# Conversion stages in separate slots of a product step, bank sums ahead of curves, and casts handed out around the bank copies

## The chip, the cores and the metric

One core of one Trainium2 chip runs the whole program in one launch. The metric is the device time of that launch in microseconds: the median of the runs. A profiled execution stands beside it, from which all rows are read.

## What is computed

Attention over 4 batches, 8 heads, 576 positions and a head size of 64, with a learned bias of the position, then two dense feed-forward blocks ("MoE" in the code) over the 2304 tokens. All weights are float64 in memory.

```python
scores = scale * q @ k^T + bias            # bias: a small MLP of log distances
x = softmax(scores) @ v                    # -> 2304 x 512
h = x @ moe_w_in                           # 512 -> 1024
solu = h * softmax(h)
x = (solu - mu) / sqrt(var + 1e-6) * g_ln @ moe_w_out      # 1024 -> 512
h = x @ moe2_w_in                          # 512 -> 2048
g = where(h >= 1, h, where(h <= -1, 0, (h + 1)**2 / 4))
out = g @ moe2_w_out                       # 2048 -> 512
```

## The kernel before

Three stages follow each other: attention (to about 355 us), the first MoE (to about 576 us), the second MoE. Every float32 operand of a matmul is split in a high and a low part, and three matmuls make one product. Each engine runs its instructions in the order in which the code emits them, and waits at the first that isn't ready; the order below is written out by hand with generators (`step(g, n)` emits the next n pieces of one).

**Conversion of the second MoE's weights** (`split_pairs`, L659). A piece is a block of 128 x 512 float64 numbers. It becomes float32 in four stages, one per `step(bw)`. Stage 1: three VectorE operations on the raw bits (L691 to L695). Stage 2: ScalarE makes the exponent (L699). Stage 3: VectorE puts in the sign (L703), one multiply makes the number (L706), and the raw load of the next piece but one is issued on SyncE (L667). Stage 4: ScalarE casts the high half (L713, L717, L726); where the piece is the second of an input pair, four VectorE subtractions (L678) make the combinations that seven products in place of eight need. Low halves and two more casts (L673, L734, L735) are kept in the list `late` and go out at the head of later stages 1 and 4 or behind a stage 2; each low half is stored to memory by SyncE. Twenty pieces (k-rows s = 0 to 4) are converted in the first MoE, with the multiply and most low halves on GpSimd; twelve (s = 5 to 7) in the second MoE, with all of it on VectorE.

**First MoE.** 18 tiles of 128 tokens. Tile i: `emit_h(i)` multiplies by w_in (24 matmuls), `split_x(i + 2)` splits a later tile's input (ScalarE L542, GpSimd L543), `emit_post(i)` is softmax and norm in steps over VectorE, ScalarE and GpSimd (L577 maximum, L578 exponential, L580 to L582, L587 squares, L589, L592 power on GpSimd, L594 and L595, the last one emitted in the next tile), `emit_lt(i - 2)` transposes (ScalarE L822, VectorE L826), `emit_o` multiplies by w_out (48 matmuls, from tile 4 on). The result of `emit_o` lies in the one PSUM buffer ps_x until ScalarE copies it to os (L842); the next tile's `emit_o` can't begin before. From tile 4 on four stages go out per tile, all ahead of `emit_o`, and odd tiles from 5 on emit four more behind it. From tile 11 on `first_x2` prepares the seven combinations of the first tokens' x2, one or two parts a tile (ScalarE L759, GpSimd L760).

**Second MoE.** 24 steps n = 0 to 23 in five legs of 5, 5, 8, 3 and 3 steps (`plan`: leg, token block p, weight row s, first and last step of a leg). A step makes seven products in the order SEQ = 1, 2, 6, 5, 7, 3, 4, six matmuls each (`emit_m`, L969), into two PSUM banks ab in turn; between them go the output matmuls of step n - 1 (`unit`, L1008, six behind each of the first six products). Four blocks 11, 22, 12, 21 of h come out of the banks: ScalarE keeps bank copies (`keep`, L935), VectorE makes the sums of 11, 22 and 12 (`summed`, tile cs, L940) behind products 2, 7 and 3. A bank is free for its next product only when its sum or copy is done. Each block then goes through `relu` (ScalarE L944), `curve` (two VectorE operations, L948 and L949) and `split_g` (ScalarE L955, VectorE L956). Before: in step n the code emits one stage in the place of product 2 (the fourth of a piece) and three in that of product 5, except in the last step of legs 0 to 3. In the place of product 3 curve 22 goes out before sum 12.

In the last step of a leg (and the first of the next) the x2 halves of the next leg are cast (L1026) and their low halves made (L1029); `sums_x2` (L1023) prepares four differences of the loaded tiles st, one after product 6 and one after product 3 in each step but the first. In a leg's first step the six result banks of the leg are copied out or added (`evac`, L988 to L993) and sent to memory, and behind that SyncE issues the loads of st (L754).

## Time and profile before

| | us |
|---|---|
| median of 3 runs | 996.57 |
| lowest, highest | 995.03, 1000.17 |
| the profiled execution | 1000.56 |
| its span, first to last instruction | 998.6 |
| TensorE busy in the span | 930.2 (93%) |
| VectorE busy | 725.9 (73%) |
| ScalarE busy | 616.8 (62%) |
| GpSimd busy | 255.2 (26%) |
| mean granted TensorE clock | 0.977 |

A matmul's end is modelled, so the share of TensorE says little by itself; what counts is where it stands idle or runs at the low clock. The clock has two levels, 1.2 and 2.4 GHz, and the granted clock of a stretch is the mean of them as a share of the higher one. "Idle before, releaser" in a row is the time that the engine stood idle ahead of an instruction and what ended it.

### The profile page before, as it was taken

To read this page: it belongs to the slowest core of one execution; us is meant where nothing else is said; L and a number is where in the kernel's file an instruction comes from. 1 tells how busy PE (TensorE), PEld (TensorE's weight loads), DVE (VectorE), ACT (ScalarE), POOL (GpSimd) and SP (SyncE) were. 2 spreads that over 40 slices of the span, in tenths; PEclk is the share of its full clock that TensorE was granted. 3 is DMA by queue.
4 is the path that set the end of the run, shared out by engine and by line. 5 is a ranking of instruction groups with operands and counts; after the bars stand their busy time and mean duration, and the time that the engine had idled before them with its cause. 6 is when DMAs were issued, how large, how long until landed. Compare 5 with 4: busy or idle time off the path is not lost.

```text
span 998.6 us, 16911 instructions
## 1 busy us (share of the span) xinstructions
PE 930.2 (93%) x6052; PEld 788.8 (79%) x6052; DVE 725.9 (73%) x1540; ACT 616.8 (62%) x1290; POOL 255.2 (26%) x229
## 2 busy tenths in 40 slices
PE   8789999999999999989989989998998899999996
PEld 4148878877788889879878977887887778888885
DVE  8988888888887367777777157787677665576764
ACT  6988888989899665666566334554445334454541
POOL 1026656565654123534464300000000000000000
PEclk9999999999999999999989989999999899999999
DMA  5893653843741002543743776849455665348442
GB/s 162 269 290 130 207 173 124 251 130 138 232 145 38 1 22 95 200 161 127 237 163 137 249 258 202 303 138 331 154 169 195 227 211 177 113 122 262 143 155 95
DMA packets 101351, 173.14 MB, mean 173 GB/s; under 512 B 10450, under 2 KB 65234, under 8 KB 101268
## 3 DMA queue, kind: packets, MB, share of 16 engines
q1 hardware_dynamic: 96000, 165.70, 50.4%
q10 hardware_dynamic: 4900, 4.72, 1.4%
q0 software_dynamic: 368, 1.64, 0.5%
q8 instruction: 48, 0.79, 0.3%
q14 instruction: 35, 0.29, 0.1%
HBM read 125.48 MB, written 46.54 MB: 172 GB/s over the span
## 4 chain that ended last, share of the span: by engine, by line
PE 37%; DVE 8%; issue 6%; POOL 5%; ACT 4%; DMA 3%; SPq 1%; ACTq 0%; POOLq 0%; DVEq 0%
PE acc L1008 14%; PE ab L969 14%; PE ps_x L837 4%; PE ps_s L559 3%; POOL wp L706 2%; PE ps_s L837 1%; DMA part_d<-ob 1%; ACT wp L699 1%; DMA st<-x_d 1%; DVE wp L703 1%; POOL xl L543 1%; DVE cs L940 1%; DVE raw L694 1%; POOL wd L673 1%; DMA pt<-part_d 1%
## 5 line engine op out<-in xcount | busy, mean ns | idle before, releaser
L1008 PE MATMUL acc<-wo,gh 128*128 128x512 f32 x576 | 181.8, 397 | 0.4 <-DVE ob L993 0.4
L421 DVE CUSTOM_DVE_ANT_0 e<-ps_s,bt 128x576 f32<-128x576 f32 x144 | 107.2, 753 | 26.8 <-PE ps_s L415 23.7
L1008 PEld LDWEIGHTS acc<-wo,gh 128*128 128x128 f32 x576 | 108.2, 191 | 15.0 <-DVE ob L993 0.8
L436 ACT ACTIVATE e<-e,su 128x576 f32<-128x576 f32 x144 | 112.1, 779 | 8.7 <-DVE su L421 7.9
L1008 PE MATMUL acc<-wo,gl 128*128 128x512 f32 x288 | 115.7, 402 | 0.0
L415 PE MATMUL ps_s<-kh,sq 128*128 128x288 f32 x320 | 102.1, 336 | 6.7 <-DVE su L421 6.3
L969 PE MATMUL ab<-x2d,wr 128*128 128x384 f32 x288 | 90.7, 356 | 12.7 <-DVE cs L940 11.8
L482 ACT COPY pt<-ps_t 128x512 f32<-128x512 f32 x144 | 83.0, 577 | 20.1 <-PE ps_t L481 19.5
L481 PE MATMUL ps_t<-ident,e 128*128 128x128 f32 x576 | 88.7, 277 | 3.1 <-ACT pt L482 2.8
L415 PE MATMUL ps_s<-kl,sq 128*128 128x288 f32 x320 | 89.9, 297 | 0.0
L944 ACT ACTIVATE ga<-cs,half_c 128x384 f32<-128x384 f32 x72 | 44.4, 617 | 72.0 <-DVE cs L940 71.2
L837 PE MATMUL ps_x<-lh,woh 128*128 128x256 f32 x256 | 75.2, 294 | 12.3 <-ACT os L842 12.3
L956 DVE TENSOR_TENSOR gl<-ga,gh 128x384 fp32r<-128x384 f32 x96 | 53.1, 553 | 42.1 <-ACT gh L955 39.8
L935 ACT COPY pk<-ab 128x384 f32<-128x384 f32 x96 | 45.4, 473 | 60.8 <-PE ab L969 60.6
L513 PE MATMUL ps_x<-pt,v 128*64 128x256 f32 x640 | 78.0, 385 | 0.6 <-ACT pt L482 0.6
L955 ACT CAST gh<-ga 128x384 fp32r<-128x384 f32 x96 | 49.3, 514 | 47.0 <-DVE ga L949 47.0
L481 PEld LDWEIGHTS ps_t<-ident,e 128*128 128x128 f32 x576 | 67.8, 141 | 12.9 <-issue 5.8
L837 PE MATMUL ps_x<-ll,woh 128*128 128x256 f32 x256 | 73.8, 288 | 0.0
L837 PE MATMUL ps_x<-lh,wol 128*128 128x256 f32 x256 | 73.7, 288 | 0.0
L948 DVE SCALAR_TENSOR_TENSOR ga<-ga 128x384 f32<-128x384 f32 x96 | 53.3, 555 | 27.2 <-ACT ga L944 25.7
L969 PEld LDWEIGHTS ab<-x2d,wr 128*128 128x128 f32 x288 | 56.4, 198 | 20.5 <-DVE cs L940 16.2
L415 PEld LDWEIGHTS ps_s<-kh,sq 128*128 128x128 f32 x320 | 61.2, 191 | 12.0 <-DVE su L421 8.3
(199 smaller groups left out, 2320.5 us busy)
## 6 DMA issues: line engine op xcount, KB each, us to landing
wr<-wi_d SPq DMA_DIRECT2D x168, 256.0 KB, 3.5
stg<-in_qk_dram SPq DMA_DIRECT2D x30, 640.0 KB, 3.9
raw<-in_w2nd_dram SPq DMA_DIRECT2D x32, 512.0 KB, 4.0
wi_d<-wd SPq DMA_DIRECT2D x24, 512.0 KB, 4.0
bias_d<-ow SPq DMA_DIRECT2D x36, 295.5 KB, 3.7
wo_d<-wd SPq DMA_DIRECT2D x16, 512.0 KB, 2.9
wo<-wo_d SPq DMA_DIRECT2D x16, 512.0 KB, 5.1
st<-x_d SPq DMA_DIRECT2D x16, 384.0 KB, 5.8
```

What stands on the lines that cost most here:

```text
L415: nc.tensor.matmul(sc[:, hf, 0:HS], lhsT=l, rhs=r, start=j == 0, stop=j == len(parts) - 1)
L421: nc.vector.tensor_tensor_reduce(out=halves(e), in0=sc[:, :, 0:HS], in1=halves(b_t[hp, n]), scale=-1.0 / float(D) ** 0.5, scalar=3.0e38, o ...
L436: nc.scalar.activation(out=e, in_=e, func=ACTF.Exp, scale=-1.0, bias=su[:, n:n + 1], accum_out=su[:, 9 + n:10 + n])
L481: nc.tensor.transpose(tp[:, kt * 128:(kt + 1) * 128], e[:, c0:c0 + 128], ident)
L482: nc.scalar.copy(out=pt[:, 4 * h:4 * h + 4, 128 * o:128 * o + 128], in_=tp.rearrange("p (a b) -> p a b", a=4))
L513: nc.tensor.matmul(x[64 * h:64 * h + 64, o0:o0 + w], lhsT=v[:, kt, 64 * h:64 * h + 64], rhs=r, start=kt == 0, stop=kt == 4, skip_group_che ...
L837: nc.tensor.matmul(ob[:, a * 256:(a + 1) * 256], lhsT=l, rhs=r[:, f, :], start=f == 0 and j == 0, stop=f == K1 - 1 and j == 2,)
L948: nc.vector.scalar_tensor_tensor(out=a, in0=a, scalar=1.0, in1=a, op0=ALU.min, op1=ALU.mult)
L955: nc.scalar.copy(out=gh, in_=a)
L956: nc.vector.tensor_tensor(out=gl, in0=a, in1=gh.bitcast(F32), op=ALU.subtract)
L969: nc.tensor.matmul(d, lhsT=l, rhs=r[:, kk], start=q in (1, 2, 5) and kk == 0 and m == 0, stop=kk == 1 and m == 2, skip_group_check=True,)
L1008: nc.tensor.matmul(d, lhsT=l, rhs=r, start=first and m == 0, stop=last and m == 2, skip_group_check=True)
```

## The change

First MoE: six stages go out per tile from tile 4 on, four ahead of `emit_o` (behind the last part of the previous norm, behind the transposes' casts, behind L582, behind the low halves of the transposes) and two behind it; the burst of odd tiles is gone. The pieces come in another order: input pairs and the first output rows first, the second output rows (s, 3) last. In `first_x2` three `yield`s move, so that no part of a tile has two long GpSimd operations, except the last.

Second MoE: a piece's four stages go out one by one: stage 1 behind sum 22 (product 7), stage 2 behind curve 12 (product 4), stage 3 behind curve 11 in the next step (product 2), stage 4 behind the split of 11 (product 5). `conv` leaves out the last steps of legs 0 to 2 for a piece's begin, so that their stages 3 and 4 are those of the step before, and a leg's first step has stages 1 and 2 alone. Sum 12 is emitted ahead of curve 22. The differences of x2 go out once a step, in leg 3 twice.

```diff
@@ first_x2
         part(7, rb, nc.gpsimd)
+        yield
         xl2[6], xh2[4], xl2[4] = slot3("c")
         part(5, ra, nc.gpsimd)
-        yield
         sub(rb, l3, ra)
         yield
         part(6, rb, nc.gpsimd)
         sub(ra, l2, rb)
         yield
+        part(4, ra, nc.gpsimd)
+        yield
         xh2[1], xh2[2], xh2[3] = slot3("d")
         part(1, l1, nc.gpsimd)
-        part(4, ra, nc.gpsimd)
         yield
         part(2, l2, nc.gpsimd)
-        yield
         part(3, l3, nc.gpsimd)
@@ first MoE, once
-            bw = split_pairs([(s, k) for s in range(NPA) for k in range(4)], wd, 4, nc.gpsimd)
+            order = [(s, k) for s in range(3) for k in range(3)] + [(s, k) for s in (3, 4) for k in (0, 1)]
+            order += [(s, 2) for s in (3, 4)] + [(s, 3) for s in range(NPA)]
+            bw = split_pairs(order, wd, 4, nc.gpsimd)
@@ first MoE, a tile
         step(lt)
         if i >= 4:
             step(bw)
-        step(bp, 2)
-        drain(lt)
         step(bp)
         if i >= 4:
             step(bw)
-        bl = bp
-        if 4 <= i < NTT - 1:
+        step(bp)
+        drain(lt)
+        if i >= 4:
             step(bw)
+        step(bp)
         if i >= 4:
             emit_o((i - 4) // 2, i % 2)
-        if i % 2 == 1 and i > 4:
-            step(bw, 4)
+            step(bw, 2)
+        bl = bp
@@ second MoE
+    def conv(n):
+        return 0 <= n < NS - 1 and (plan[n][0] > 2 or not plan[n][4])
...
                     relu((n, 11))
-                    if n > 0 and swap != 0:
+                    curve((n, 11))
+                    if conv(n - 1):
                         step(bw)
-                    curve((n, 11))
...
                 split_g((n, 11))
-                if swap != 0:
-                    step(bw, 3)
+                if conv(n - 1):
+                    step(bw)
...
                 relu((n, 22))
+                if conv(n):
+                    step(bw)
             elif q == 3:
+                summed((n, 12), d, k_t[6])
                 curve((n, 22))
-                summed((n, 12), d, k_t[6])
                 split_g((n, 22))
                 relu((n, 12))
-                if not head:
+                if not head and g == 3:
                     step(xs)
             else:
                 c_t[n, 21] = keep(d)
                 curve((n, 12))
+                if conv(n):
+                    step(bw)
```

What this does to an engine's queue is seen at three places. VectorE, step 1 of the second MoE, from the split of block 11 on, before (L940 are sums 22 and 12, L948 and L949 curve 22, the rest a conversion's low half, stages 1 and 3):

```order
L956 TENSOR_TENSOR gl<-ga,gh 128x384
L673 TENSOR_TENSOR wd<-wp_7005,wd 128x512
L691 TENSOR_SCALAR wp_7150<-raw_6953 128x512
L694 SCALAR_TENSOR_TENSOR raw_6953<-raw_6953,wp_7150 128x512
L695 TENSOR_SCALAR wp_7150<-raw_6953 128x512
L703 SCALAR_TENSOR_TENSOR wp_7150<-raw_6953,wp_7150 128x512
L706 TENSOR_TENSOR wp_7150<-raw_6953,wp_7150 128x512
L940 TENSOR_TENSOR cs<-ab_6948,pk 128x384
L948 SCALAR_TENSOR_TENSOR ga<-ga 128x384
L949 TENSOR_TENSOR ga<-ga,cs 128x384
L940 TENSOR_TENSOR cs<-ab_6947,pk 128x384
```

The same place in the changed kernel, where the lines of the second MoE are two higher (L942 are the sums):

```order
L958 TENSOR_TENSOR gl<-ga,gh 128x384
L942 TENSOR_TENSOR cs<-ab_6948,pk 128x384
L673 TENSOR_TENSOR wd<-wp_7019,wd 128x512
L691 TENSOR_SCALAR wp_7170<-raw_6953 128x512
L694 SCALAR_TENSOR_TENSOR raw_6953<-raw_6953,wp_7170 128x512
L695 TENSOR_SCALAR wp_7170<-raw_6953 128x512
L942 TENSOR_TENSOR cs<-ab_6947,pk 128x384
L950 SCALAR_TENSOR_TENSOR ga<-ga 128x384
L951 TENSOR_TENSOR ga<-ga,cs 128x384
```

Sum 22 now follows the split, the conversion's first stage stands between the two sums, its third has left, and curve 22 stands behind sum 12. ScalarE in tile 8 of the first MoE, from the end of the tile before to the bank copy os, before:

```order
L726 CAST wd_5312<-wp_5299 128x256
L542 CAST xh<-xb_1419 128x512
L578 ACTIVATE eb,stb<-ps_s,stb 128x1024
L594 ACTIVATE stb<-stb 128x1
L595 ACTIVATE scb<-scb,stb 128x1024
L822 CAST lh<-ps_t 128x4x128 x2
L699 ACTIVATE wp_5354<-wp_5354,exp_c 128x512
L734 CAST wd<-wd 128x512
L735 CAST wd<-wd 128x512
L587 ACTIVATE eb,stb<-scb,stb 128x1024
L713 CAST wd<-wp_5354 128x512
L842 COPY os<-ps_x 128x512
```

And in the changed kernel:

```order
L713 CAST wd<-wp_5247 128x512
L542 CAST xh<-xb_1419 128x512
L578 ACTIVATE eb,stb<-ps_s,stb 128x1024
L594 ACTIVATE stb<-stb 128x1
L595 ACTIVATE scb<-scb,stb 128x1024
L822 CAST lh<-ps_t 128x4x128 x2
L699 ACTIVATE wp_5358<-wp_5358,exp_c 128x512
L587 ACTIVATE eb,stb<-scb,stb 128x1024
L717 CAST wd<-wp_5358 128x512
L842 COPY os<-ps_x 128x512
L843 DMA x_d<-os 128x2x256
L699 ACTIVATE wp_5448<-wp_5448,exp_c 128x512
```

The two casts L734 and L735 have left this tile, a piece's cast still stands ahead of os, and the next piece's exponent stands behind it. GpSimd in the same tile, before (L706 multiplies, L543 and L673 low halves, L592 the norm's power):

```order
L706 TENSOR_TENSOR wp_5299<-raw_5121,wp_5299 128x512
L543 TENSOR_TENSOR xl<-xb_1419,xh 128x512
L592 TENSOR_TENSOR stb<-stb,mhalf 128x1
L706 TENSOR_TENSOR wp_5354<-raw_5243,wp_5354 128x512
L543 TENSOR_TENSOR xl<-xb_1419,xh 128x512
```

And changed:

```order
L706 TENSOR_TENSOR wp_5247<-raw_5115,wp_5247 128x512
L543 TENSOR_TENSOR xl<-xb_1419,xh 128x512
L673 TENSOR_TENSOR wd<-wp_5247,wd 128x512
L706 TENSOR_TENSOR wp_5358<-raw_5222,wp_5358 128x512
L592 TENSOR_TENSOR stb<-stb,mhalf 128x1
```

The tile's multiply has moved ahead of the norm's power, with a low half ahead of it.

## Rows read from the trace of the kernel before

**Rows 1.** The page's first part: busy us, share of the span, instructions of each engine.

```profile
PE 930.2 (93%) x6052; PEld 788.8 (79%) x6052; DVE 725.9 (73%) x1540; ACT 616.8 (62%) x1290; POOL 255.2 (26%) x229
```

**Rows 2.** The chain that ended last: start us, us, what it was.

```profile
415.17 5.45 PE ps_s L559 x24
...
652.77 1.39 PE acc L1008 x6
...
902.31 2.08 PE ab L969 x12
```

**Rows 3.** Stretches of steps: length, busy (instructions) by engine, PEclk, DMA share, GB/s.

```profile
575.84:588.28 12.44, 8.73 (x44) 7.91 (x43) 7.12 (x13) 4.77 (x10) 0.00 (x0) 0.87 0.56 187
588.28:641.72 53.44, 50.08 (x234) 43.29 (x235) 39.57 (x73) 22.72 (x45) 0.00 (x0) 0.97 0.77 264
641.72:657.47 15.75, 15.75 (x78) 14.02 (x79) 11.57 (x19) 8.93 (x17) 0.00 (x0) 1.00 0.77 257
657.47:747.84 90.37, 83.80 (x391) 72.20 (x391) 68.89 (x125) 43.21 (x83) 0.00 (x0) 0.96 0.61 201
747.84:840.52 92.68, 84.96 (x391) 73.57 (x391) 63.27 (x113) 39.80 (x77) 0.00 (x0) 0.94 0.61 200
840.52:887.44 46.92, 46.92 (x235) 42.04 (x235) 26.54 (x47) 20.74 (x39) 0.00 (x0) 1.00 0.42 134
503.00:552.00 49.00, 42.41 (x259) 38.79 (x259) 36.27 (x66) 32.65 (x55) 26.57 (x20) 0.90 0.41 150
```

**Rows 4.** TensorE's waits, whole span: us in total, times, longest us.

```profile
PE ab L969 <- DVE cs L940: 19.9, 17, 3.7
PE ps_x L837 <- ACT os L842: 12.3, 5, 4.6
```

**Rows 5.** Timeline, TensorE in step 1: products 7, 4, then product 1 of step 2.

```profile
599.72 1.21 PE L969 MATMUL ab<-x2b,wr 128*128 128x384 f32 x6
...
604.87 1.33 PE L969 MATMUL ab<-x2c,wr 128*128 128x384 f32 x6
607.24 0.44 PE L969 MATMUL ab<-x2d,wr 128*128 128x384 f32 x1 [1.04 <-DVE cs L940]
```

**Rows 6.** Timeline, VectorE in step 1, from product 7 on.

```profile
599.93 0.68 DVE L673 TENSOR_TENSOR wd<-wp,wd 128x512 fp32r<-128x512 f32 x1
...
602.93 0.69 DVE L703 SCALAR_TENSOR_TENSOR wp<-raw,wp 128x512 uint32<-128x512 uint32 x1 [0.79 <-ACT wp L699]
...
604.27 0.55 DVE L940 TENSOR_TENSOR cs<-ab,pk 128x384 f32<-128x384 f32 x1
...
606.63 0.55 DVE L940 TENSOR_TENSOR cs<-ab,pk 128x384 f32<-128x384 f32 x1
```

**Rows 7.** Timeline, VectorE in steps 4 to 6, where legs change.

```profile
647.82 0.95 DVE L1029 TENSOR_TENSOR x2a<-st,x2d 128x768 fp32r<-128x768 f32 x1
...
663.01 0.42 DVE L678 TENSOR_TENSOR wd<-wd,wp 128x256 f32<-128x256 f32 x1
...
676.82 0.69 DVE L993 COPY ob<-acc 128x512 f32<-128x512 f32 x1 [1.03 <-DMA part_d<-ob]
...
686.12 0.96 DVE L1023 TENSOR_TENSOR st<-st,st 128x768 f32<-128x768 f32 x1 [2.77 <-DMA st<-x_d]
```

**Rows 8.** Timeline, GpSimd and ScalarE at the end of tile 8.

```profile
432.89 0.93 POOL L592 TENSOR_TENSOR stb<-stb,mhalf 128x1 f32<-128x1 f32 x1 [8.13 <-DVE stb L589]
433.79 1.37 POOL L706 TENSOR_TENSOR wp<-raw,wp 128x512 f32<-128x512 f32 x1
435.19 0.62 ACT L713 CAST wd<-wp 128x512 fp32r<-128x512 f32 x1 [2.57 <-POOL wp L706]
435.72 0.58 ACT L842 COPY os<-ps_x 128x512 f32<-128x512 f32 x1
```

**Rows 9.** Timeline, GpSimd and VectorE at the end of tile 7.

```profile
416.65 1.30 POOL L706 TENSOR_TENSOR wp<-raw,wp 128x512 f32<-128x512 f32 x1
416.71 1.79 DVE L694 SCALAR_TENSOR_TENSOR raw<-raw,wp 128x512 f32<-128x512 uint32 x1
```

**Rows 10.** The page's DMA issues: KB each, median us to landing.

```profile
raw<-in_w2nd_dram SPq DMA_DIRECT2D x32, 512.0 KB, 4.0
```

## The prediction

> **What bounds the kernel now.** I read the busy line of the page first, then the span cut at step starts, then TensorE's waits, then single steps in order of time. TensorE is busy 930.2 of 998.6 us [rows 1], so what can be gained is its idle time and the time at the low clock. A product of the second MoE is six matmuls, 1.04 us (2.08 for twelve); the output matmuls between two products are six, 1.39 us [rows 2]. A step is seven products and six such gaps: 7 x 1.04 + 6 x 1.39 = 15.62 us. Steps 15 to 17 convert nothing and take 46.92 / 3 = 15.64 us at clock 1.00 [rows 3]; that is the floor.
>
> Against it [rows 3]: step 0, which has no output matmuls, takes 12.44 where 7 x 1.04 = 7.28 would do: 5.16 over. Steps 1 to 3: 53.44 - 46.92 = 6.52 over. Step 4, a leg's last, converts nothing: 0.11. Steps 5 to 9: 90.37 - 78.20 = 12.17. Steps 10 to 14: 92.68 - 78.20 = 14.48. Together **38.4 us** over the floor, and each such row but step 4's has a clock below 1.00, so part of it is matmuls at 1.2 GHz behind a stall. TensorE's waits name VectorE's bank sum (cs, L940): 19.9 us in 17 waits [rows 4]. The second entry there that this change can reach is the first MoE's bank copy os: 12.3 us in 5 waits. Tiles around the largest ran at mean clock 0.90 for 49 us [rows 3], 4.9 us of clock; about 1 of it fell into idle time, I take 4. **First MoE: 16.3 us.** Both together: 54.7 us.
>
> Why the sums are late: in step 1 the fifth product in order, number 7, starts at 599.72 and ends near 600.9 [rows 5], so the sum "22" could run at 601. It starts at 604.27 [rows 6]: VectorE first does a low half (599.93), stage 1 up to 602.14, an idle 0.79 for ScalarE's exponent, stage 3 (602.93, then the multiply). Product 4 needs that sum and starts late at 604.87. Then the curve of 22, with a wait for ScalarE's relu in it, holds VectorE until 606.63, where sum "12" starts, though its product ended before 603.4; product 1 of step 2 waits 1.04 for it [rows 5, 6].
>
> **The change part by part, second MoE.**
> *Sum 12 ahead of curve 22.* From the end of sum 22 (604.82) to 606.63 are 1.81 us of curve and waiting [rows 6] that no longer stand ahead of sum 12. Nothing is added; the curve's own readers, the output matmuls of block 22, come behind two products of the next step, some 4 us later.
> *Stages apart.* Stage 1 now stands after sum 22, stage 2 after the seventh product, stage 3 after curve 11, stage 4 after the split of 11. The instructions are the same. Count a step from its start. Product 7 ends at 10.76, product 3 at 13.19, product 4 must start at 14.58, the next step's product 1 at 15.62. I follow VectorE through the heaviest kind, stage 4 with four subtractions (0.42 each [rows 7], 1.7 together): sum 11 4.2, curve 11 6.1, stage 3 (602.93 to 604.27 [rows 6], 1.34) 7.5, a sum of x2 halves (0.95, as the halves of [rows 7]) 8.4, low half of 11 10.0, subtractions 11.7, sum 22 12.25 (limit 14.58), a low half of 256 columns and stage 1 (together up to 2.2, 599.93 to 602.14 in [rows 6]) 14.2 to 14.5, sum 12 14.8 to 15.0 (limit 15.62). It fits, with 0.6 to 0.8 to spare. The next step begins with VectorE and ScalarE behind, and by the same count ends its sum 12 at about 15.2, still inside. Steps 1 to 3: 6.52 becomes 0.3.
> *Step 0.* Stages 3 and 4 have gone from it, and stage 1 stands behind sum 22: that sum ends 0.2 after product 4 could start; stage 1 (1.6 us) then delays sum 12 and product 1 of step 1 by about 1.1. 5.16 becomes 1.3, and I expect no low clock behind it: the waits of that size in steps 1 to 3 left 0.97, which is the end of step 0's low spell.
> *A leg's last step* pays: steps 4 and 9 now carry stages 3 and 4 beside four low halves of x2 (0.95 each [rows 7]) and one sum of x2 halves. In step 4 stage 4 is the kind with subtractions: VectorE starts some 1.8 behind, and the count gives sum 22 at 15.85 (1.27 late) and sum 12 another 0.5 late: 0.11 becomes 1.8. Step 9 has only a cast there: 0.3.
> *A leg's first step and the one behind it.* Before, stages 1 to 3 stood ahead of the copies of finished banks; the last ones waited for a result buffer's DMA (676.82, 1.03), the loads of x2 left after them, and at 686.12 VectorE waited 2.77 for those, with a split, stages and sum 22 queued behind it [rows 7]. Now only stage 1 is in the first step, after sum 22; the copies are no longer behind a piece's 4 us of stages (599.93 to 604.27 in [rows 6]), so buffers are free in time and the loads can issue some 3 us earlier in their step. What is late next: the last bank copy behind curve 22 (0.3), ScalarE's exponent and two casts ahead of the next step's bank copy (0.5 to 1.0). With step 9, steps 5 to 9 keep 2.4 and steps 10 to 14 1.4.
> *x2 sums once a step* instead of twice: the four sums fit the four steps ahead of their use; nothing on the path.
> *SyncE.* Raw loads leave behind stage 3, later than before within a piece, the stores of low halves follow their instructions; weight blocks queue behind both. No wait of TensorE for a weight block shows, and twelve blocks are held ahead, 1.7 steps: cost 0, or, without that cover, up to a landing, 4.0 [rows 10], per wait.
>
> After: 1.3 + 0.3 + 1.8 + 2.4 + 1.4 = 7.2, and one spell of low clock, priced as in step 0's row, 0.13 x 12.44 = 1.6 [rows 3]: 8.8. **Gain 38.4 - 8.8 = 29.6.** Bounds: none of the residue, 38.4; twice it, 20.8.
>
> **First MoE.** os may come as late as the next tile's 5.45 us of input matmuls [rows 2] and its transposes last. In tile 8 it comes at 435.72: GpSimd does the norm's power (432.89, 0.93), then the multiply 433.79, then ScalarE's cast 435.19 for which it had waited 2.57, then os [rows 8]. The change puts the multiply ahead of the power and leaves the odd tiles' burst of four stages out; two stages stand behind os instead, and have those 6 us. The tightest tiles are 5, 7, 9, 11: an exponent and two casts (0.62 each, as in [rows 8]) stand ahead of os, which then comes about at the limit. The x2 parts move by a tile at most; tile 17 has one more of the long GpSimd halves, with over 20 us of matmuls behind it. I take 2.5 us left of 16.3; bounds 0 and all of it. **Gain 13.8.**
> What works against it: beside a GpSimd multiply (416.65, 1.30) a VectorE conversion took 1.79 [rows 9], where the same kind without GpSimd, in the second MoE, fits with two others into 1.6 us (up to 602.14) [rows 6]. That is about 1.1 lost each time the two meet, and stages spread over a tile can meet oftener. The Trainium skill, "SBUF — State Buffer", section "Who interferes with whom", says that a VectorE instruction with two inputs in SBUF and a GpSimd one that reads SBUF exclude each other for a whole instruction; by that rule the odd tiles, which have no room, would wait again, and the trace agrees as far as this one pair shows.
>
> **Sum.** 29.6 + 13.8 = 43.4. The profiled execution was 1000.56 us, its span 998.6 and 2.0 around it: 957.2 after. The median of the runs is 996.57, 4.0 below: 996.57 - 43.4 = **953**.
>
> **Rivals.**
> *GpSimd collisions keep the first MoE's waits.* Two meetings in a tile (2.2 us) use up the odd tiles' room, os is late in seven tiles by about 1 to 2 us and the clock drops once or twice; the gain of 13.8 is gone: 996.6 - 29.6 = 967. For it: rows 9; against: nine of fourteen tiles wait for nothing today with more work ahead of os. 0.10.
> *ScalarE takes VectorE's place.* An exponent and a cast or two now stand ahead of the next step's relu and bank copy; if each of the twelve converting steps loses 1.2 us to it, 14.4 come back: 968. Against: by the count above the copy ends just before product 6 needs it. 0.10.
> *Nothing of the residue shows*: 54 us gained, 943. 0.06.
> *It does not do what it says*: the sums are late for another reason than the queue and all stays within 0.5%. Rows 6 leave no gap between stage 3 and sum 22. 0.03.
> *Slower: stage 1 waits for its raw weights between sums 22 and 12*, and stops sum 12, curves and splits with it. Each load has from stage 3 of one step to stage 1 of the next but one, 15.6 + 7.3 = 22.9 us, against landings of 4.0 [rows 10]; it decides from about 27 us, and at 28 us twelve steps would lose 4.2 each, 50: 953 + 50 = 1003. For it: nothing in these rows. 0.03.
> *Forecast*, 946 to 960: 0.68.
>
> The range takes the forecast, the full gain and the first rival: 943 to 967. Faster by over 0.5% (5 us, about what a measurement of this kernel can tell from no change): 0.94; within: 0.03; slower: 0.03.
>
> **What would show it.** Right: converting steps of 15.6 to 15.9 us, sum 12 next to its product's end, hardly an entry of cs in TensorE's waits; step 0 near 8.6 us; step 4 longer than 15.75; copies and x2 loads of step 5 and 10 without DMA waits on VectorE; entries of os under 3 us; clock near 1.00 from 400 us on. Wrong: steps 1 to 3 over 16.5 us with pk or cs as releaser, os waits over 6 us, or a stage 1 idle on a DMA.

## The result, and the profile after

| | before | after |
|---|---|---|
| median of 4 runs, us | 998.37 | 947.68 |
| lowest, highest | 995.03, 1002.48 | 946.11, 947.94 |
| ratio, 95% interval | | 0.9487 [0.9446, 0.9528] |
| span of the profiled execution | 998.6 | 945.6 |
| mean granted TensorE clock | 0.977 | 0.995 |

The forecast was 953 us in a range of 943 to 967; it came out 5.3 us lower, inside the range. TensorE, 93% busy before [rows 1], is now 96% busy. First the page's busy line of the kernel after, then two stretches (columns as in [rows 3]), of after and then of before. The first MoE is taken from TensorE's first matmul with w_out (L837, in tile 4) to the first matmul of the second MoE, and the second MoE from there to the end:

```profile
PE 911.2 (96%) x6052; PEld 778.7 (82%) x6052; DVE 723.8 (77%) x1540; ACT 610.9 (65%) x1290; POOL 255.2 (27%) x229
```

```profile
372.21:559.89 187.68, 187.51 (x1300) 173.93 (x1298) 138.97 (x250) 119.48 (x206) 89.89 (x70) 1.00 0.53 183
559.89:945.60 385.71, 377.26 (x1874) 336.88 (x1872) 287.25 (x515) 182.09 (x356) 0.00 (x0) 1.00 0.64 210
```

```profile
371.18:575.84 204.66, 192.34 (x1300) 177.52 (x1298) 138.80 (x250) 119.31 (x206) 89.92 (x70) 0.97 0.48 168
575.84:998.60 422.76, 392.96 (x1874) 343.99 (x1872) 290.67 (x515) 188.16 (x356) 0.00 (x0) 0.97 0.58 192
```

The first MoE became 16.98 us shorter and the second 37.05; what lies ahead is 1.03 longer (372.21 and 371.18), and that difference is there before the changed code begins. Together 53.0, the difference of the spans. In the first MoE TensorE is busy for 187.51 of 187.68 us: by this row nothing is left to gain there by order. VectorE has as much work there as before (138.97 and 138.80).

The second MoE by steps of the kernel after, in the same groups as [rows 3] (step 0; 1 to 3; 4; 5 to 9; 10 to 14; steps 15 to 17 take 46.92 us as before):

```profile
559.89:568.32 8.43, 7.76 (x44) 7.15 (x42) 4.68 (x10) 3.59 (x7) 0.00 (x0) 1.00 0.77 251
568.32:615.40 47.08, 47.08 (x234) 42.23 (x235) 38.97 (x73) 22.02 (x46) 0.00 (x0) 1.00 0.84 279
615.40:631.79 16.39, 15.81 (x80) 13.92 (x79) 14.41 (x26) 9.22 (x18) 0.00 (x0) 1.00 0.92 320
631.79:710.21 78.42, 78.42 (x391) 70.30 (x392) 67.42 (x123) 42.01 (x82) 0.00 (x0) 1.00 0.69 231
710.21:788.72 78.51, 78.47 (x391) 70.24 (x391) 61.63 (x112) 37.92 (x76) 0.00 (x0) 1.00 0.73 238
```

Against the floor of 7.28 and 15.64 us a step, 2.6 us are left of 38.4: 1.15 in step 0, 0.16 in steps 1 to 3, 0.75 in step 4, 0.22 and 0.31 in the ten others. Steps 0 to 14 are 228.83 us long, where they were 264.68: 35.85 shorter. The clock stands at 1.00 in every row.

TensorE's waits after (us in total, times, longest), the two that answer to [rows 4]:

```profile
PE ab L971 <- DVE cs L942: 1.2, 2, 0.7
...
PE ps_x L837 <- ACT os L842: 0.2, 1, 0.2
```

Seventeen waits for a bank sum became two (0.67 and 0.58 us), and five for os became one of 0.2. VectorE in step 2 after, from sum 22 to sum 12 and on (timeline: start, us; compare [rows 6]):

```profile
595.53 0.55 DVE L942 TENSOR_TENSOR cs<-ab,pk 128x384 f32<-128x384 f32 x1
596.00 0.41 DVE L673 TENSOR_TENSOR wd<-wp,wd 128x256 fp32r<-128x256 f32 x1
...
597.52 0.43 DVE L695 TENSOR_SCALAR wp<-raw 128x512 uint32<-128x512 uint32 x1
597.86 0.55 DVE L942 TENSOR_TENSOR cs<-ab,pk 128x384 f32<-128x384 f32 x1
598.33 0.55 DVE L950 SCALAR_TENSOR_TENSOR ga<-ga 128x384 f32<-128x384 f32 x1
```

Between the sums stand a low half (L673) and stage 1 (L691, L694, L695) and nothing else; curve 22 (598.33) comes behind. Sum 12 ends at 598.41, and product 1 of step 3, which needs it, starts at 599.76. That looks like 1.35 us to spare. Two experiments below show that it is less than half of that.

### The profile page after: what moved, and what is told of

Read it like the earlier page. It is cut to its first block, busy times and chain, and to the rows that moved or that the text cites. A ratio compares the mean times of both kernels' runs of the same rounds, so it can differ in the third digit from the quotient of the medians.

```text
span 945.6 us, 16893 instructions
## 1 busy us (share of the span) xinstructions
PE 911.2 (96%) x6052; PEld 778.7 (82%) x6052; DVE 723.8 (77%) x1540; ACT 610.9 (65%) x1290; POOL 255.2 (27%) x229
## 4 chain that ended last, share of the span: by engine, by line
PE 48%; DVE 6%; ACT 3%; issue 2%; POOL 1%; DMA 1%; SPq 0%; ACTq 0%; DVEq 0%
PE acc L1010 19%; PE ab L971 17%; PE ps_x L837 5%; PE ps_s L559 5%; PE ps_s L837 1%; POOL wp L706 1%; PE ps_t L818 1%; DVE wp L703 1%; DVE raw L694 1%; DMA pt<-part_d 1%; DVE wp L695 1%; ACT eb L578 1%; ACT wp L699 0%; DVE wd L678 0%; DVE cs L942 0%
## 5 line engine op out<-in xcount | busy, mean ns | idle before, releaser
L1010 PE MATMUL acc<-wo,gh 128*128 128x512 f32 x576 | 179.4, 392 | 0.3 <-DVE ob L990 0.2
L1010 PEld LDWEIGHTS acc<-wo,gh 128*128 128x128 f32 x576 | 105.8, 188 | 15.2 <-DVE ob L990 1.0
L971 PE MATMUL ab<-x2d,wr 128*128 128x384 f32 x288 | 84.9, 335 | 1.2 <-DVE cs L942 1.2
L946 ACT ACTIVATE ga<-cs,half_c 128x384 f32<-128x384 f32 x72 | 44.4, 616 | 61.6 <-DVE cs L942 61.6
L837 PE MATMUL ps_x<-lh,woh 128*128 128x256 f32 x256 | 73.4, 287 | 0.2 <-ACT os L842 0.2
L837 PE MATMUL ps_x<-lh,wol 128*128 128x256 f32 x256 | 72.1, 282 | 0.0
L837 PE MATMUL ps_x<-ll,woh 128*128 128x256 f32 x256 | 72.1, 282 | 0.0
L942 DVE TENSOR_TENSOR cs<-ab,pk 128x384 f32<-128x384 f32 x72 | 39.9, 554 | 40.0 <-PE ab L971 40.0
L216 POOL TENSOR_TENSOR kl<-stg,kh 128x576 fp32r<-128x576 f32 (+1 forms) x30 | 47.6, 1586 | 81.0 <-DVE kh L213 60.9
```

The lines of the kernel that those rows point to most:

```text
L216: eng.tensor_tensor(out=kl, in0=ks, in1=kh.bitcast(F32), op=ALU.subtract)
L837: nc.tensor.matmul(ob[:, a * 256:(a + 1) * 256], lhsT=l, rhs=r[:, f, :], start=f == 0 and j == 0, stop=f == K1 - 1 and j == 2,)
L971: nc.tensor.matmul(d, lhsT=l, rhs=r[:, kk], start=q in (1, 2, 5) and kk == 0 and m == 0, stop=kk == 1 and m == 2, skip_group_check=True,)
L1010: nc.tensor.matmul(d, lhsT=l, rhs=r, start=first and m == 0, stop=last and m == 2, skip_group_check=True)
```

## The experiments

The first MoE is measured below as above, and a step from its first matmul to that of the next. Steps 15 to the end, which convert nothing, vary from 156.9 to 158.5 us between the executions of all kernels here, in no order that the edits explain; so parts of the second MoE are compared by steps 0 to 14 (after: 228.8).

**Each half of the change alone.** The second MoE of the kernel after behind the first MoE of the kernel before; against the kernel after the edit is

```diff
@@ first MoE, once
-            order = [(s, k) for s in range(3) for k in range(3)] + [(s, k) for s in (3, 4) for k in (0, 1)]
-            order += [(s, 2) for s in (3, 4)] + [(s, 3) for s in range(NPA)]
-            bw = split_pairs(order, wd, 4, nc.gpsimd)
+            bw = split_pairs([(s, k) for s in range(NPA) for k in range(4)], wd, 4, nc.gpsimd)
...
@@ first MoE, a tile (and first_x2's three yields as before)
+        step(bp, 2)
+        drain(lt)
         step(bp)
...
         if i >= 4:
             emit_o((i - 4) // 2, i % 2)
-            step(bw, 2)
-        bl = bp
+        if i % 2 == 1 and i > 4:
+            step(bw, 4)
```

> The first MoE of before with the second MoE of after. Theory (the two parts gain by themselves, each by its engine queues): the second MoE's part of the gain, 37 us of the 53 in the two traces, stays: ratio about 0.963, 961 us where before is 998; TensorE's waits for os stay near 12 us, those for cs fall to 1 or 2 us. Rival (the parts help each other: with an untouched first MoE the second starts late or its weights come late): over 970 us.

Measured: 967.45 us, ratio 0.9699 [0.9668, 0.9730]. Steps 0 to 14 took 228.8, as in the kernel after; the first MoE took 206.1, and TensorE waits there much as in the kernel before (12.3 us in 5 [rows 4]):

```profile
PE ps_x L837 <- ACT os L842: 14.1, 6, 4.6
```

The other half: the first MoE of the kernel after ahead of the second MoE of the kernel before.

```diff
@@ second MoE, as before
                     relu((n, 11))
-                    curve((n, 11))
-                    if conv(n - 1):
+                    if n > 0 and swap != 0:
                         step(bw)
+                    curve((n, 11))
...
                 split_g((n, 11))
-                if conv(n - 1):
-                    step(bw)
+                if swap != 0:
+                    step(bw, 3)
...
-                summed((n, 12), d, k_t[6])
                 curve((n, 22))
+                summed((n, 12), d, k_t[6])
```

> The first MoE of after with the second MoE of before. Theory: the waits for os vanish and only the 16 to 17 us of the first MoE are gained: ratio about 0.983, 981 us where before is 998; waits for cs stay near 20 us. Rival (GpSimd collisions or something else of the first MoE gives part of it back when the second MoE is slow): over 988 us.

Measured: 983.01 us, ratio 0.9854 [0.9812, 0.9896]. The first MoE took 187.5, with no wait for os in TensorE's list; steps 0 to 14 took 262.5, and the waits for the sums are back: 19.2 us in 16. So the halves are worth 3.0% and 1.5%, and the whole 5.1%, or 4.9% in a second comparison. Each half gives the length that its stage has in the whole, to 0.2 us: neither leans on the other.

The second comparison is the kernel after once more, on another chip, so that its variants below stand beside it:

> The changed kernel itself, as the reference for the others of this call: 946 to 949 us.

Measured: 949.53 us, ratio 0.9512 [0.9486, 0.9538]; the first MoE took 187.5.

**Sum 12 ahead of curve 22, alone, in the kernel before.**

```diff
             elif q == 3:
-                curve((n, 22))
                 summed((n, 12), d, k_t[6])
+                curve((n, 22))
                 split_g((n, 22))
```

> Before, with one edit: the sum of block 12 is emitted ahead of the curve of block 22; stages stay three in the place of product 5. Theory (two causes in the queue: the curve ahead of sum 12, worth the waits of 1.04 us, and three stages ahead of sum 22, worth the rest): the waits of 1.04 us at product 1 go, 11 of them, and with them some of the low clock, but the waits at product 4 in steps 0, 6, 10 and 11 stay: 10 to 20 us gained, ratio 0.98 to 0.99. Rival 1 (the order of the sums is all of it): 35 us gained. Rival 2 (the stages' place is all of it, sum 12 only inherits the lateness of sum 22): under 4 us gained.

Measured: 985.47 us, ratio 0.9884 [0.9854, 0.9914]. Steps 0 to 14: 248.3, 16.4 less than before. The waits for sums fell from 19.9 to 8.1 us, 5 of them, and all 5 are of product 4 for sum 22. Step 0 of this kernel, VectorE and then TensorE:

```profile
585.85 0.69 DVE L703 SCALAR_TENSOR_TENSOR wp<-raw,wp 128x512 uint32<-128x512 uint32 x1 [0.79 <-ACT wp L699]
586.58 0.69 DVE L706 TENSOR_TENSOR wp<-raw,wp 128x512 f32<-128x512 f32 x1
587.19 1.02 DVE L940 TENSOR_TENSOR cs<-ab,pk 128x384 f32<-128x384 f32 x2
```

```profile
587.79 1.83 PE L969 MATMUL ab<-x2c,wr 128*128 128x384 f32 x6 [3.72 <-DVE cs L940]
```

Stage 3 with its wait for the exponent stands ahead of sum 22, and product 4 waits 3.72 us for it. One moved line gives 16.4 of the 35.85 us; the other 19.4 need the stages apart. It also brings up another wait: for VectorE's copies of result banks TensorE now waits 4.0 us in two places, where it waited 0.4 before. The two causes that the prediction named for the second MoE are both there, and each has its own waits.

**The kernel after with curve 22 ahead of sum 12 again.**

```diff
             elif q == 3:
-                summed((n, 12), d, k_t[6])
                 curve((n, 22))
+                summed((n, 12), d, k_t[6])
                 split_g((n, 22))
```

> After, with one edit undone: the curve of block 22 is again emitted ahead of the sum of block 12; stages stay apart. Theory: sum 12 is then about 1.2 us and stage 1 behind sum 22 and reaches its limit in the converting steps: in after it ends 1.3 to 1.5 us ahead of product 1, the curve takes 1.2 and now waits for the relu: 0 to 0.5 us per converting step, 2 to 8 us lost against after, 950 to 956 us. Rival 1 (the order of the sums is all of it): over 970 us. Rival 2 (the stages' place is all of it): within 1 us of after.

Measured: 953.41 us, ratio 0.9558 [0.9530, 0.9587]; steps 0 to 14: 233.8, 5.0 more than after. The time came out as expected, its place did not: steps 2 and 3, which convert, still take 15.64. The loss sits in step 0 (9.49), step 1 (17.33), step 4 (17.29) and in small parts in steps 9 to 11. VectorE and TensorE at the end of step 0:

```profile
566.13 0.55 DVE L950 SCALAR_TENSOR_TENSOR ga<-ga 128x384 f32<-128x384 f32 x1
...
567.19 0.55 DVE L942 TENSOR_TENSOR cs<-ab,pk 128x384 f32<-128x384 f32 x1
```

```profile
567.80 0.44 PE L971 MATMUL ab<-x2d,wr 128*128 128x384 f32 x1 [1.73 <-DVE cs L942]
```

The curve takes 1.06 us of VectorE (566.13 to 567.19) and the stall, 0.67 in the kernel after, is 1.73. Behind it the clock fell to its lower level, 1.2 GHz: the granted clock is 0.50 from 568.69 to 572.11, which costs 1.7 of the 5.0 us. So with the stages apart a step without other load carries the curve too; the order of the two is needed where a step has none to spare. It is worth 16.4 us in the kernel before and 5.0 in the kernel after. Read the other way, the stages apart without it take steps 0 to 14 from 264.7 to 233.8, 30.9 us (with the differences of x2 once a step, which were not tried alone): each of the two causes hides part of the other, and their shares depend on which is removed first.

**How much room a converting step has.** Dummy additions of 128 x 384 on VectorE between sums 22 and 12 in the twelve steps that begin a piece, 0 to 3, 5 to 8 and 10 to 13 (nothing reads their result): first three in a step, 1.4 us, as they start 0.47 apart.

```diff
                 relu((n, 22))
                 if conv(n):
                     step(bw)
+                    if n < 14:
+                        junk = wc.tile([128, XT], F32, tag="junk", name="junk", bufs=1)
+                        for _ in range(3):
+                            nc.vector.tensor_tensor(out=junk, in0=c_t[n, 22], in1=c_t[n, 22], op=ALU.add)
```

> After, with three more additions on VectorE (128x384, 0.56 us each, 0.47 from one to the next: 1.4 us, results unused) between sum 22 and sum 12 in steps 0 to 13 where a piece is begun, 12 steps. Theory (the room there is what the trace of after shows: sum 12 ends 1.3 to 1.5 us ahead of its limit, since instructions that don't depend on each other overlap by 0.1 us): nearly all of it is hidden in the steady steps; step 0 has no room and takes 1.4 more, the others 0 to 0.3: 2 to 4 us over after, 949 to 952 us. Rival (the prediction's count, which leaves 0.6 to 0.8 us of room and the next step with less): 0.7 us and more in every one of 12 steps, and low clock behind some: over 957 us.

Measured: 963.73 us, ratio 0.9652 [0.9627, 0.9676]; steps 0 to 14: 242.3, 13.5 more. The theory, which read the 1.35 us to spare from step 2, fell; the prediction's count (0.6 to 0.8) was the rival, and came nearer, without the low clock that it named. Then one addition in a step:

```diff
+                    if n < 14:
+                        junk = wc.tile([128, XT], F32, tag="junk", name="junk", bufs=1)
+                        nc.vector.tensor_tensor(out=junk, in0=c_t[n, 22], in1=c_t[n, 22], op=ALU.add)
```

> After, with one addition on VectorE (0.47 us in its row) between sum 22 and sum 12 in each of the same 12 steps; three of them cost 14 us of the 16.9 us that they add. Theory A (VectorE is all but the bound of the converting steps, so its work is paid for nearly in full): 4 to 5 us over after, 953 to 955 us. Theory B (there is room of about 0.5 us a step, and only what exceeds it is carried from step to step): step 0 pays 0.5, the others nothing, 949 to 951 us.

Measured: 952.38 us, ratio 0.9540 [0.9508, 0.9572]; steps 0 to 14: 230.7, 1.9 more. Steps 2 and 3 with three additions, and then step 2 with one (step 3 has 15.64 too):

```profile
588.03:604.22 16.19, 16.00 (x78) 13.96 (x78) 14.71 (x30) 6.69 (x14) 0.00 (x0) 1.00 0.78 261
604.22:620.82 16.60, 16.07 (x78) 13.88 (x79) 14.11 (x27) 7.97 (x16) 0.00 (x0) 1.00 0.61 206
```

```profile
587.72:603.36 15.64, 15.64 (x79) 14.05 (x79) 13.48 (x28) 6.73 (x14) 0.00 (x0) 1.00 0.86 292
```

With one addition (0.47 us) steps 1 to 3, 5, 7, 8, 10, 12 and 13 are as long as without. Steps 0, 6 and 11 are 0.46 longer each. In step 0 sum 12 was late already; in steps 6 and 11 TensorE waits (0.23 and 0.50) for the copy of the last result bank, which VectorE makes behind curve 22 of steps 5 and 10, and so behind the addition there. Step 4 has none of its own and is 0.46 longer (16.85): the lag of step 3 is carried into it, for its first VectorE instruction starts 0.59 into the step, in place of 0.12. Three additions cost steps 2, 3, 7, 8 and 10 between 0.55 and 0.97, 0.82 in the mean: 1.41 - 0.82 leaves 0.6 us of room in a step, 0.45 to 0.86 in single ones (steps 12 and 13 have 1.0). Step 6, with a wait of 0.78 for that copy and one of 1.50 for sum 12, is 2.8 longer. Step 9, which has no addition, is 0.74 longer. The 1.35 of a single step is more than that, since what stands behind the sums (a curve, splits, ScalarE's casts for both) then also comes later, and the next step begins behind.

**The two waits that are left.** Step 0's stage 1 and, in a leg's last step, one low half of x2 go behind sum 12.

```diff
                 relu((n, 22))
-                if conv(n):
+                if conv(n) and n > 0:
                     step(bw)
             elif q == 3:
                 summed((n, 12), d, k_t[6])
+                if n == 0:
+                    step(bw)
+                if swap == 0:
+                    lo2(5, st_t[5], nc.vector)
                 curve((n, 22))
...
-                lo2(xq, st_t[xq], nc.vector)
+                if q != 7:
+                    lo2(xq, st_t[xq], nc.vector)
```

> After, with two edits: in step 0 stage 1 goes out behind sum 12 in place of ahead of it, and in a leg's last step the low half of x2's part 5 goes out behind sum 12. Theory (the two waits for cs that are left, 0.67 us into step 1 and 0.58 us into step 5, come from VectorE doing these ahead of sum 12; in step 4 it even waits 1.47 us for ScalarE's cast of part 5): both go, about 1.2 us less than after, no entry for cs above 0.3 us. Rival (the sums are late for the lag that VectorE carries over from earlier steps): the waits stay above 0.4 us each and the time is that of after.

Measured: 949.15 us, ratio 0.9507 [0.9483, 0.9531], the time of the kernel after. The two waits did go: step 0 takes 7.59, step 4 15.64. But product 2 of step 1 now waits for a ScalarE bank copy:

```profile
572.00 0.45 PE L971 MATMUL ab<-x2d,wr 128*128 128x384 f32 x1 [0.96 <-ACT pk L937]
```

Step 1 takes 16.87 (15.80) and step 5 16.08 (15.81): 1.59 gained, 1.34 given back. The next edit moves, besides, step 0's stage 2 (ScalarE's exponent) into step 1, to ask whether that is what holds the copy up.

```diff
@@ on top of the edit above
                     split_g((n - 1, 12))
+                if n == 1:
+                    step(bw)
                 load_wo(n)
...
                 curve((n, 12))
-                if conv(n):
+                if conv(n) and n > 0:
                     step(bw)
```

> The version with sums ahead of stage 1 in step 0 and of x2's last low half in a leg's last step, in which the wait for cs had turned into one of 0.96 us for a bank copy on ScalarE, with one more edit: stage 2 of step 0 goes out in step 1 behind the first bank copy and the split of block 12. Theory (ScalarE's exponent, which waits for the late stage 1, stood ahead of the bank copy): the wait for pk goes too, step 1 takes 15.7 us, about 1 us less than that version and 1.5 less than after. Rival (the copy is late for another reason, such as the order of relu and copy): the wait for pk stays at 0.9 us.

Measured: 948.41 us, ratio 0.9503 [0.9476, 0.9529]; step 1 takes 16.81, and the wait stays, 0.91. The exponent was not the cause. ScalarE around it:

```profile
571.21 0.51 ACT L957 CAST gh<-ga 128x384 fp32r<-128x384 f32 x1 [2.62 <-DVE ga L951]
...
572.15 0.46 ACT L937 COPY pk<-ab 128x384 f32<-128x384 f32 x1
```

ScalarE stands idle for 2.62 us until VectorE has made curve 22, which now comes behind stage 1; its cast and a relu (L946, 571.63) are queued ahead of the copy that frees the bank. Sum 12 is early and the copy behind the curve is late. None of these versions is measurably faster than the kernel after.

**The first MoE in parts.** Four things changed there: where the four stages ahead of `emit_o` stand, the burst of four behind odd tiles (two behind every tile instead), the order of pieces, and the x2 parts. The first three were put back one at a time in the kernel after; the x2 parts were not tried alone. The old places, without the burst:

```diff
         if i >= 4:
             step(bw)
+        step(bp, 2)
+        drain(lt)
         step(bp)
         if i >= 4:
             step(bw)
-        step(bp)
-        drain(lt)
-        if i >= 4:
+        bl = bp
+        if 4 <= i < NTT - 1:
             step(bw)
-        step(bp)
         if i >= 4:
             emit_o((i - 4) // 2, i % 2)
             step(bw, 2)
-        bl = bp
```

> After, with the first MoE's four stages ahead of the bank copy put back to the places of before (the third and fourth behind the norm's power), two stages behind it in every tile as in after, no burst in odd tiles. Theory (the burst was the cause of the waits for os: it delays the next tile's maximum on VectorE and its whole norm): os comes about 1 us later in its tile than in after and TensorE waits under 3 us for it: 947 to 952 us. Rival (the place of the multiply and cast, behind the power, is the cause): waits of 8 us and more, 957 to 965 us.

Measured: 954.94 us, ratio 0.9572 [0.9545, 0.9599]; the first MoE takes 194.0, 6.5 more, with 4.5 us in 8 waits for os: between the theory's time and the rival's. (A wait delays the next matmul by more than its row gives, 0.94 against 0.67 behind step 0 of the kernel after; eight times 0.27 is about the rest, an estimate.) ScalarE at the end of tile 9 in this kernel:

```profile
444.01 0.72 ACT L699 ACTIVATE wp<-wp,exp_c 128x512 int32<-128x512 int32 x1 [2.08 <-DVE wp L695]
...
445.67 0.57 ACT L842 COPY os<-ps_x 128x512 f32<-128x512 f32 x1
```

The exponent waits 2.08 us for stage 1 on VectorE, and os stands behind it and two casts, as L734 and L735 in the kernel after. The new places with the burst:

```diff
             emit_o((i - 4) // 2, i % 2)
-            step(bw, 2)
+            step(bw, 4 if i % 2 == 1 and i > 4 else 0)
```

> After, with one edit in the first MoE: the two stages behind every tile's output matmuls become four behind odd tiles' (the burst of before); the four slots ahead of them stay as in after. With the last run, which had the old slots and no burst and took 5 us more than after (waits for os 4.5 us), this splits the first MoE's gain. Theory (the burst is the larger cause, the slots the smaller): waits for os of 6 to 11 us and some low clock, 957 to 964 us. Rival (only both together make the waits): under 3 us of waits, within 3 us of after.

Measured: 953.08 us, ratio 0.9548 [0.9520, 0.9575]; the first MoE takes 193.0, 5.5 more. The theory (6 to 11 us of waits for os) fell, and so did the rival (within 3 us of after): there is one such wait, and the rest is another wait and clock. TensorE in that stretch, and the stretch at the low level:

```profile
537.54 0.66 PE L818 MATMUL ps_t<-ident,scb 128*128 128x128 f32 x4 [1.35 <-DVE ll L826]
539.40 0.58 PE L837 MATMUL ps_x<-lh,woh 128*128 128x256 f32 x1 [1.20 <-ACT os L842]
```

```profile
538.70:545.52 6.82, 6.12 (x28) 6.12 (x29) 1.29 (x2) 5.34 (x9) 6.35 (x5) 0.50 0.40 149
```

Two waits of 2.55 us together, and 6.12 us of matmuls at half the clock, of which half, 3.1, is lost: 5.6. The old order of pieces:

```diff
-            order = [(s, k) for s in range(3) for k in range(3)] + [(s, k) for s in (3, 4) for k in (0, 1)]
-            order += [(s, 2) for s in (3, 4)] + [(s, 3) for s in range(NPA)]
-            bw = split_pairs(order, wd, 4, nc.gpsimd)
+            bw = split_pairs([(s, k) for s in range(NPA) for k in range(4)], wd, 4, nc.gpsimd)
```

> After, with the first MoE's pieces in the order of before (per row s: both input halves, then both output rows). Theory (the order decides in which tile stage 4 with its four subtractions, and the two late casts, meet the bank copy, and nothing else): waits for os of 0 to 3 us, 947 to 953 us. Rival (with six stages a tile the order is what keeps the casts behind the copies): waits of 6 us and more, over 956 us.

Measured: 953.19 us, ratio 0.9547 [0.9516, 0.9579], whose interval touches that of the kernel after; in the profile the first MoE takes 191.6, 4.1 more, with 2.4 us for os and 1.2 for the transposes (0.65 for the norm's last step on ScalarE, 0.54 for their bank). That is the upper edge of the theory. So no single part makes the gain: put back alone they cost 6.5, 5.5 and 4.1, together 16.1, and all of them with the x2 parts 18.6 (206.1 against 187.5).

## Why the prediction was right, and where it missed

**Sum 12 and the stages apart, steps 1 to 3: right.** 0.3 was forecast, 0.16 measured. Both causes were shown apart (alone, the sum's place gives 16.4 us, the stages 30.9; both 35.85). The count of 0.6 to 0.8 us to spare came close to the 0.60 of the run with three additions, and in part by luck: it puts the end of sum 12 at 14.8 to 15.0 in the heaviest step, and in step 2 that end lies at 14.29 (598.41, from 584.12). The count adds each record in full, which makes it late, and about as much is lost again because a step's lag goes on into the next.

**Step 0: right.** 1.3 was forecast, 1.15 measured: product 4 starts 0.14 late (566.34), and product 1 of step 1 0.94 (568.32), behind a stall for sum 12 that its row gives as 0.67; stage 1 stands between the sums, from 566.20 to 567.81. No low clock follows, as forecast.

**Step 4: the size and the cause were wrong.** 1.8 was forecast, in two parts: sum 22 late by 1.27 behind subtractions and halves, and sum 12 by 0.5. VectorE and TensorE there after:

```profile
619.24 0.55 DVE L942 TENSOR_TENSOR cs<-ab,pk 128x384 f32<-128x384 f32 x1
...
621.55 0.69 DVE L703 SCALAR_TENSOR_TENSOR wp<-raw,wp 128x512 uint32<-128x512 uint32 x1
...
627.42 0.95 DVE L1031 TENSOR_TENSOR x2c<-st,x2e 128x768 fp32r<-128x768 f32 x1
628.29 0.55 DVE L942 TENSOR_TENSOR cs<-ab,pk 128x384 f32<-128x384 f32 x1
630.31 0.96 DVE L1031 TENSOR_TENSOR x2e<-st,x2b 128x768 fp32r<-128x768 f32 x1 [1.47 <-ACT x2b L1028]
631.18 0.55 DVE L942 TENSOR_TENSOR cs<-ab,pk 128x384 f32<-128x384 f32 x1
```

```profile
630.00 1.21 PE L971 MATMUL ab<-x2c,wr 128*128 128x384 f32 x6
631.79 0.44 PE L971 MATMUL ab<-x2d,wr 128*128 128x384 f32 x1 [0.58 <-DVE cs L942]
```

Sum 22 (628.29 to 628.84) is over a microsecond ahead of product 4 at 630.00. It ended 13.44 after the step's start, where the count gave 15.85. Two terms of that count failed. The larger is the lag of 1.8 that VectorE was to start with: sum 11 ends 4.39 into the step (619.24 + 0.55, from 615.40), against 4.2 in the count of the heaviest step, so the lag is 0.2. The smaller is the sum of durations: it added every record in full, but an operation that doesn't need the last one's result starts some 0.1 us before that one's end (628.29 against 627.42 + 0.95 = 628.37). The twelve records from 621.55 to the end of sum 22 add up to 7.96 us and take 7.29. What is late is sum 12, behind a low half of x2 that waits 1.47 us for ScalarE's cast, with VectorE idle. The cast itself is queued on ScalarE behind the relu that needs sum 22. The forecast looked for VectorE's work and found the right sum by another cause, which is luck. The edit that put this half behind sum 12 took the wait away (step 4 at 15.64), which confirms it.

**Steps 5 to 14: the mechanism right, the residue mis-sized.** 2.4 and 1.4 were forecast, 0.22 and 0.31 measured. The copies of result banks no longer wait for a buffer's DMA (they did for 1.03 us [rows 7]), and the wait for the loads of x2 shrank but did not vanish as forecast:

```profile
657.46 0.96 DVE L1025 TENSOR_TENSOR st<-st,st 128x768 f32<-128x768 f32 x1 [0.63 <-DMA st<-x_d]
736.18 0.96 DVE L1025 TENSOR_TENSOR st<-st,st 128x768 f32<-128x768 f32 x1 [1.87 <-DMA st<-x_d]
```

Before it was 2.77 in the first place [rows 7] and 3.31 in the second; 0.63 and 1.87 reach no product. Of the two terms for a late copy, the last result bank's behind curve 22 (0.3) is what is left in step 11 (15.96 us). VectorE's copy and the output matmul that needs the bank:

```profile
727.04 0.68 DVE L995 COPY ob<-acc 128x512 f32<-128x512 f32 x1
```

```profile
727.78 0.73 PE L1010 MATMUL acc<-wo,gh 128*128 128x512 f32 x2
```

The copy ends at 727.72, and the matmul, which would have followed the one before at about 727.58, starts behind it. The other term (0.5 to 1.0 for ScalarE's exponent and casts) did not show; it is mis-sized in both legs, and with it the residue. That ScalarE stands next is seen in the two edits to the last waits of the second MoE, where a bank copy of its is late by 0.9 as soon as a curve moves back.

**The clock: 1.6 us were set aside, none was lost.** In steps 0 to 14 of the kernel before, the clock was at its lower level for 23.9 us (584.93 to 591.76, 694.16 to 700.99, 765.84 to 769.25, 786.32 to 793.15), with 21.2 us of matmuls in them, so about 10.6 of the 35.85 us are clock. With 6.2 us less left over than the 8.8 of the forecast, the second MoE is most of the miss.

**First MoE: 2.5 us left was too careful.** 13.8 was forecast, 16.98 measured, 0.2 us of waiting for os left; besides, TensorE's busy time fell by 4.83 us (192.34 to 187.51), where the forecast took 4 for the clock. ScalarE in tile 9 after, the kind of tile named as "about at the limit":

```profile
442.03 0.71 ACT L699 ACTIVATE wp<-wp,exp_c 128x512 int32<-128x512 int32 x1
...
443.68 0.57 ACT L842 COPY os<-ps_x 128x512 f32<-128x512 f32 x1
```

The exponent and the two casts (L734 at 442.64, L735 at 443.16) wait for nothing; os is done at 444.25, and TensorE's next `emit_o` starts at 444.55 without a wait: 0.3 us inside. The queue is the one that the prediction listed; with the old places the same copy stood at 445.67 behind an exponent that waited for VectorE. In tile 8, whose cast waited 2.57 us for GpSimd's multiply [rows 8], the cast (428.50) waits for nothing. The prediction took the burst and the multiply's place for the causes; the runs add the order of pieces (4.1 us), to which it gave no term.

**Rivals.** *GpSimd collisions*: its premise is half true, its price is not. In the first MoE the four conversion operations cost 2.79 us a piece before and 3.08 after, 5.8 us for twenty pieces, so these meet GpSimd for longer; but VectorE's busy time in the stage is the same (138.80 and 138.97), since others got shorter (three differences of x2, L768, from 1.66 us each to 0.95), the tiles have room for it, and no wait follows. *ScalarE takes VectorE's place*: not in this version; two small edits of it show that it stands next, with 0.9 us. *Nothing of the residue shows* (943) is what the profile came near to, with 2.8 of 54.7 us left; the time lies in the forecast's own range, 946 to 960. *It does not do what it says* and *raw loads hold up stage 1* are out: no stage 1 of the second MoE waits for a DMA. (A raw load has 20.3 us there, issued at 591.54 and first read at 611.81, and not the 22.9 of the prediction; landings of 3.8 leave room for either.)

**The arithmetic of the miss.** 6.2 more in steps 0 to 14, 3.2 in the first MoE, 1.2 in the last steps, less 1.03 in attention: 9.6 by the profiled executions (the last two are within what these parts vary between executions). By the medians it is 5.3, since the forecast took the gain of one profiled execution off a median: that execution of before took 1000.56, 4.0 more than the 996.57, and that of after 947.47, 0.2 less than its median. So the forecast number lies closer than the sum of its parts, by luck.

## What to carry to other kernels

Where an engine with a queue in order makes both the results that free another engine's buffers and work of its own, put the freeing results first, and hand the rest out in pieces no longer than the room ahead of the next such result. Measure that room with dummy work in every step, a small and a larger amount: the gap in front of one consumer in one step overstates it (1.35 against 0.60 us here). And when a move takes a wait away, look at what the moved work was ahead of: here 1.59 us gained at two places came back as 1.34 at two others.

## What the runs showed of the hardware that was not expected

**The collision moved to another instruction.** VectorE's costliest conversion operations in the first MoE (busy us, mean ns of one), after and then before:

```profile
L695 DVE TENSOR_SCALAR wp<-raw 128x512 uint32<-128x512 uint32 x20 | 19.2, 962 | 0.7
...
L694 DVE SCALAR_TENSOR_TENSOR raw<-raw,wp 128x512 f32<-128x512 uint32 x20 | 15.0, 749 | 1.2
```

```profile
L694 DVE SCALAR_TENSOR_TENSOR raw<-raw,wp 128x512 f32<-128x512 uint32 x20 | 20.0, 1001 | 1.5 <-DVE wp L691 0.5
...
L695 DVE TENSOR_SCALAR wp<-raw 128x512 uint32<-128x512 uint32 x20 | 11.1, 552 | 0.7
```

And one such meeting in the kernel after, GpSimd and VectorE:

```profile
429.31 1.57 POOL L673 TENSOR_TENSOR wd<-wp,wd 128x512 fp32r<-128x512 f32 x1
```

```profile
429.76 1.40 DVE L695 TENSOR_SCALAR wp<-raw 128x512 uint32<-128x512 uint32 x1
```

L695 reads one tile and takes 0.43 us alone; where a GpSimd instruction had begun before it, it took 1.40 and ended just behind that one (431.16 against 430.88), in eleven cases of twenty, where the kernel before has two. L694 took 1.6 us and more in six cases before and in one after. The prediction had looked only at L694, an operation with two inputs in SBUF [rows 9]. The Trainium skill, "SBUF — State Buffer", section "Who interferes with whom", says that a `tensor_scalar` can run in a mode that uses both port pairs where its operands allow it, and that then whichever of it and GpSimd issues first has the shared pair for its whole instruction and the other blocks; the 1.40 us agree.

**The same stall costs clock in one execution and not in another.** The kernel before and the version in which only the second MoE is changed run the same code in the first MoE, and TensorE stalls there for 2.80 us at the same place. The stall, and a stretch behind it, in the kernel before:

```profile
436.35 0.39 PE L837 MATMUL ps_x<-lh,woh 128*128 128x256 f32 x1 [2.80 <-ACT os L842]
```

```profile
436.35:446.35 10.00, 10.00 (x67) 9.27 (x68) 7.26 (x14) 6.97 (x12) 5.27 (x5) 1.00 0.65 236
```

And in the other:

```profile
438.31 0.39 PE L837 MATMUL ps_x<-lh,woh 128*128 128x256 f32 x1 [2.80 <-ACT os L842]
```

```profile
439.65:443.06 3.41, 3.41 (x19) 3.41 (x18) 2.44 (x7) 3.38 (x7) 2.27 (x2) 0.50 0.99 378
```

In the first the granted clock stays at 1.00; in the second it is 0.50 for 3.41 us, half of which is lost. The length of a stall does not tell the two cases apart in these traces. Stalls of 1.48 us (curve 22 first, into step 5) and 2.32 us (three additions, into step 1) left the clock at 1.00; one of 1.73 (curve 22 first, into step 1) was followed by 0.50 for 3.42 us, and 1.35 and 1.20 close together by 0.50 for 6.82. What a stall costs in clock has to be read from the granted clock behind it; what decides it these runs do not show.
